# Multiply behind the reciprocal, keys' bias, a relu and a low half of the Strassen visits placed elsewhere in a fused attention and mixture-of-experts kernel

## The chip, the cores and the metric

The kernel runs on one core of a Trainium2 chip. The metric is the device time of one execution in microseconds; the median of the runs is compared. TensorE is the matmul engine, VectorE (DVE), ScalarE (ACT) and GpSimd (POOL) work on tiles, and SyncE (SP) issues most of the loads and stores.

## The reference

```python
def phi(x):                                    # x scaled by D ** -0.25
    h = einsum('bhsd,md->bhsm', x, omega) - sum(x * x, -1) / 2
    return exp(h - max(h, -1)) / sqrt(m)
q_p, k_p = phi(q), phi(k)                      # 4 batches, 8 heads, 576 tokens, 64 wide, 128 features
kv, z = einsum('bhsm,bhsd->bhmd', k_p, v), sum(k_p, 2)
x = (q_p @ kv) / (q_p @ z + 1e-6)              # 2304 tokens x 512
out = 0
for e in range(4):                             # 4 experts, 1024 hidden
    out += p[:, e] * (relu(x @ w1[e]) @ w2[e]) # p: domain_probs, normalised over the experts
```

## The kernel before

Every product of the second half is made of three matmuls in fp32r: an operand is split into a high half (rounded, by ScalarE, line 492) and a low half (the difference, by GpSimd or VectorE, line 495), and high x high, high x low and low x high are added up in a PSUM bank. `w1sh`/`w1sl`, `w1ah`/`w1al` and `w2h`/`w2l` are such pairs of weights, `xbh`/`xbl` of activations, `hh`/`hl` of the hidden layer after the relu.

The work is a list of visits (a slice of tokens, an expert and a half of its hidden units). The first slice is visited plainly (`plain`); two more slices of 896 tokens are visited eight times each by a Strassen form (`fast`): seven products `p1` to `p7` of half-blocks for each of two groups g of hidden units. Product sums live in PSUM banks (`u`, `b2`, `b5`); `keep` copies one out (line 852), and `both` adds a product to a kept sum on VectorE (line 857), applies the relu on ScalarE (`hh`, line 862) and makes the low half on VectorE (`hl`, line 863). Products 4, 6 and 7 are added onto the same bank `u`, so each waits until the reader of the one before is through. The eight visits of the last slice are deep (`DEEP`): the second layer too is done by seven products (`sevens`), with sums of w2 (`w2f`, made by `w2_sides` on GpSimd, lines 540 to 543, and split into `w2s`) and sums of hidden blocks (`t1`, `t2`, `r11`, on VectorE and GpSimd, split into `T` and, for the last, into further columns of `hs`, which the profile shows as `hl<-va,hh`).

The attention of the first batch is done ahead. That of the others, one pair of heads (`Halves`) after the other, is interleaved as steps of a generator (`later_ticks`): between parts of a visit the next step is emitted, and each engine executes what was emitted for it strictly in that order. A pair's keys are projected (`project`, `project_tails`), their maxima taken on VectorE (`maxima`, `maxima_tails`), from these and the sums of squares (`lengths`, whose squares GpSimd makes) the bias is formed (`bias`, lines 289 and 290, `nbk`), and ScalarE takes the exponentials (`exp`, `exp_tails`). These free the banks for the projection of the queries. The pair before is finished meanwhile: `numerators` (matmuls and copies to `nu` and `dn`) and `divide`, a reciprocal on VectorE (line 365) and a multiply on GpSimd into `raw_x` (line 367), the input of the expert layers.

Weights are loaded by SP into rings of few buffers (line 488); a load waits until GpSimd has made the low half of what stood in the buffer, and the loads of keys and queries (line 247) stand in the same queue behind them.

Of the kernel before, what the change touches and what calls it, by code (L numbers as in the profile page):

```python
# [14 lines left out]
def attention_moe(ctx, tc, kT, qT, kd, qd, kn, qn, vn, omT, probs, w1, w2, out):  # L15
# [10 lines left out]
    nc = tc.nc  # L26
# [42 lines left out]
    def f32(ap):  # L69
        return ap.bitcast(F32)  # L70
# [167 lines left out]
    class Halves(Pair):  # L238
# [121 lines left out]
                nc.scalar.activation(nu[own], ps[j][own], AF.Copy)  # L360
            self.num[part] = nu, dn, n

        def divide(self, part):
            nu, dn, n = self.num.pop(part)
            nc.vector.reciprocal(dn, dn)
            for o, c, m in in_ring(self.b * S + 2 * P * part, n):
                nc.gpsimd.tensor_tensor(raw_x[:, place(self.hp), c:c + m], nu[:, o:o + m], dn[:, o:o + m], ALU.mult)

# [16 lines left out]
    def later_ticks(pairs, over):  # L385

        before = None
        for p, then in zip(pairs, pairs[1:] + [None]):
            p.project("k")
            p.project_tails("k")  # L390
            p.maxima("k")
            p.maxima_tails("k")
            if before:
                before.numerators(0)
            yield
            p.bias("k")
            p.exp_tails("k")
            p.exp("k", 0)
            p.lengths("q")
            if before:  # L400
                before.divide(0)
            yield
            p.exp("k", 1)
            if before:
                before.numerators(1)
            yield
            p.project("q")
            p.project_tails("q")
            p.maxima("q")
            p.maxima_tails("q")  # L410
            p.bias("q")
            if before:
                before.divide(1)
            yield
            p.exp_tails("q")
            p.exp("q", 0)
            if then:
                then.load("k")
            yield
            p.exp("q", 1)  # L420
            if then:
                then.load("q")
            yield
            p.sum_keys()
            if then:
                then.load_v()
                if then.hp == 0:
                    then.load_tails()
                then.square("k")
            yield  # L430
            p.turn(0)
            if over and then:
                then.square("q")
            yield
            p.turn(1)
            if then:
                if over:
                    then.lengths("k")
                else:
                    then.square("q")  # L440
            yield
            if over and then:
                before = p
                continue
            before = None
            p.numerators(0)
            if then:
                then.lengths("k")
            yield
            p.divide(0)  # L450
            p.numerators(1)
            yield
            p.divide(1)
            yield

    def visit(u, n, c0, m):
# [333 lines left out]
    def start_sides2(v):  # L790
        B = {}
        g = w2_sides(v, B)
        next(g)
        sides2[v] = B, g
# [5 lines left out]
    def fast(v):  # L800
# [31 lines left out]
        def first_rows(t):  # L832
            return t[:, :WT]
# [17 lines left out]
            P_[g][name] = t = held([P, 512], "sum", F32)[:, :n]  # L851
            nc.scalar.activation(t, P_[g][where], AF.Copy)  # L852

        def both(g, f, j, where, name):
            ha, hc = (x[:, j * n:(j + 1) * n] for x in hs[2 * g + f])
            t = P_[g][name]
            nc.vector.tensor_tensor(t, P_[g][where], t, ALU.add)  # L857
            if deep and g == 0 and j == 1:
                if f == 0:
                    less(t1[:, 0], last_rows(t), r11[:, 0])  # L860
                t, ha, hc = (x[:, :n - WT] for x in (t, ha, hc))
            nc.scalar.activation(ha, t, AF.Relu)  # L862
            nc.vector.scalar_tensor_tensor(hc, t, 0.0, f32(ha), ALU.max, ALU.subtract)  # L863
            if deep and g == f == j == 0:
                nc.scalar.activation(r11[:, 0], first_rows(t), AF.Relu)

# [5 lines left out]
            product(g, 2, "b2")  # L872

        def sum2(g):
            both(g, 0, 0, "b2", "p1")

        def p5(g):
            product(g, 5, "b5")
# [10 lines left out]
        def p4(g):  # L889
            product(g, 4, "u", start=False)  # L890
            ha, hc = (x[:, :n] for x in hs[2 * g + 1])
            nc.scalar.activation(ha, P_[g]["u"], AF.Relu)  # L892
            nc.vector.scalar_tensor_tensor(hc, P_[g]["u"], 0.0, f32(ha), ALU.max, ALU.subtract)  # L893

        def p3(g):
# [16 lines left out]
        def sevens():  # L912
# [32 lines left out]
            for q in QS3:  # L945
                seventh(q, X[q][:, R], sums_of(5), mixed(1, R), start=False)
            split(r11, *T[7], nc.scalar, nc.gpsimd)
            next(ready, None)
            less(t1[:, 0], first_rows(P_[1]["p1"]), t2[:, 0])
            for q in QS3:  # L950
# [77 lines left out]
            keep_sides(v)  # L1028
        p4(0)
        if deep:  # L1030
            nc.scalar.activation(r11[:, 1], first_rows(P_[0]["u"]), AF.Relu)
            less(t1[:, 1], last_rows(P_[0]["p5"]), r11[:, 1])
            p6(1)
            split(t1, *T[5], nc.scalar, nc.gpsimd)
            if v == DEEP[0]:
                start_sides2(v + 1)
            next(ready, None)
            yield from sevens()
            return
        prepare()  # L1040
        p6(1)
        next(more, None)
        next(ready, None)
        begun(0)
        p7(1)
# [304 lines left out]
```

## Time and profile before

| | |
|---|---|
| median of the runs | 907.02 us (906.31, 907.02 and one of 1774.53) |
| profiled execution, its own time | 907.93 us |
| its span, first to last instruction | 906.2 us |
| mean granted clock of TensorE | 0.996 |
| busy: TensorE matmul, VectorE, ScalarE, GpSimd | 894.8, 581.6, 477.4, 533.4 us |

Times in the rows below are microseconds from the start of the span. A matmul's end is modelled and matmuls overlap, so the distance between two starts tells more than a row's width. In brackets stands the idle time of the engine before an instruction and what released it. L numbers are lines of the kernel before.

### The profile page before, as it was taken

How to read it: one execution, taken by the hardware profiler on the slowest of the kernel's cores; microseconds unless marked ns; L12 is line 12 of the kernel's file. 1: busy time of each engine (PE TensorE's matmuls, PEld its weight loads, DVE VectorE, ACT ScalarE, POOL GpSimd, SP SyncE). 2: the span in 40 equal slices, each digit the busy share in tenths (PEclk: the TensorE clock that was granted, in tenths of full speed). 3: DMA queues.
4: the chain of work that ended last, by engine and by line, in shares of the span. 5: the costliest groups of instructions: out<-in, count | busy, mean ns of one | idle time of the engine just before them, and what ended most of it. 6: DMA issues, size and time to landing. Idle time of an engine off the chain costs nothing.

```text
span 906.2 us, 14545 instructions
## 1 busy us (share of the span) xinstructions
PE 894.8 (99%) x5340; PEld 796.5 (88%) x5340; DVE 581.6 (64%) x985; ACT 477.4 (53%) x1077; POOL 533.4 (59%) x476
## 2 busy tenths in 40 slices
PE   9999999999999999999999999999999999999998
PEld 9888888888778888888888889888899999999998
DVE  5665567766568755474766474776756856857757
ACT  6454677776564555444455444464454544544541
POOL 4756465655534452433534333448889888898783
PEclk9999999999989999999999999999999999999999
DMA  7673444444421645234325324156333334244212
GB/s 178 162 230 118 134 157 146 152 134 155 137 70 45 214 125 180 82 117 133 117 80 194 106 92 152 59 187 209 123 110 127 113 98 152 81 130 151 82 59 82
DMA packets 57447, 117.21 MB, mean 129 GB/s; under 512 B 9824, under 2 KB 19744, under 8 KB 57376
## 3 DMA queue, kind: packets, MB, share of 16 engines
q1 hardware_dynamic: 52528, 99.21, 34.5%
q0 software_dynamic: 4608, 16.78, 5.4%
q8 instruction: 42, 0.69, 0.3%
q10 hardware_dynamic: 240, 0.30, 0.1%
q14 instruction: 29, 0.24, 0.1%
HBM read 94.77 MB, written 21.50 MB: 128 GB/s over the span
## 4 chain that ended last, share of the span: by engine, by line
PE 85%; DVE 8%; ACT 2%; issue 2%; DMA 1%; POOL 1%; SPq 0%; DVEq 0%; ACTq 0%; POOLq 0%
PE g L846 26%; PE g L910 11%; PE g L673 9%; PE g L675 9%; PE g L674 9%; PE g L658 3%; PE g L659 3%; PE g L660 3%; PE kv L314 2%; PE k_ps L266 1%; DVE hl L863 1%; DVE sum L857 1%; PE q_ps L266 1%; PE qt_ps L325 1%; PE k_ps L148 1%
## 5 line engine op out<-in xcount | busy, mean ns | idle before, releaser
L495 POOL TENSOR_TENSOR w2l<-w2r,w2h 128x512 fp32r<-128x512 f32 x93 | 120.8, 1307 | 103.7 <-ACT w2h L492 74.2
L692 DVE SCALAR_TENSOR_TENSOR acc<-g,pr,acc 128x256 f32<-128x256 f32 (+1 forms) x219 | 126.3, 603 | 45.6 <-PE g L675 31.5
L673 PE MATMUL g<-w2h,hh 128*128 128x512 f32 x344 | 138.4, 402 | 0.6 <-ACT hh L892 0.4
L675 PE MATMUL g<-w2h,hl 128*128 128x512 f32 x344 | 135.3, 393 | 0.0
L674 PE MATMUL g<-w2l,hh 128*128 128x512 f32 x344 | 135.1, 393 | 0.0
L863 DVE SCALAR_TENSOR_TENSOR hl<-sum,hh 128x448 fp32r<-128x448 f32 (+1 forms) x96 | 61.4, 639 | 105.9 <-ACT hh L862 105.9
L495 POOL TENSOR_TENSOR w1al<-w1r,w1ah 128x256 fp32r<-128x256 f32 (+1 forms) x77 | 82.6, 1089 | 48.9 <-ACT w1ah L492 45.6
L495 POOL TENSOR_TENSOR w1sl<-w1r,w1sh 128x512 fp32r<-128x512 f32 (+1 forms) x43 | 74.4, 1732 | 60.2 <-ACT w1sh L492 52.0
L862 ACT ACTIVATE hh<-sum 128x448 fp32r<-128x448 f32 (+1 forms) x96 | 50.2, 523 | 93.1 <-DVE sum L857 93.1
L846 PE MATMUL g<-xbh,w1sh 128*128 128x448 f32 x256 | 94.6, 370 | 1.5 <-ACT sum L852 1.5
L857 DVE TENSOR_TENSOR sum<-g,sum 128x448 f32<-128x448 f32 x96 | 59.5, 620 | 56.1 <-PE g L846 55.8
L846 PE MATMUL g<-xbl,w1sh 128*128 128x448 f32 x256 | 93.7, 366 | 0.0
L846 PE MATMUL g<-xbh,w1sl 128*128 128x448 f32 x256 | 93.6, 366 | 0.0
L852 ACT ACTIVATE sum<-g 128x448 f32<-128x448 f32 x96 | 51.7, 540 | 60.8 <-PE g L846 60.2
L675 PEld LDWEIGHTS g<-w2h,hl 128*128 128x128 f32 x344 | 65.0, 189 | 15.3 <-DVE hl L893 0.7
L673 PEld LDWEIGHTS g<-w2h,hh 128*128 128x128 f32 x344 | 65.2, 189 | 13.9 <-ACT hh L892 0.9
L674 PEld LDWEIGHTS g<-w2l,hh 128*128 128x128 f32 x344 | 65.2, 189 | 11.4
L846 PE MATMUL g<-xbh,w1ah 128*128 128x448 f32 x192 | 70.8, 369 | 0.7 <-DVE sum L857 0.7
L846 PE MATMUL g<-xbh,w1al 128*128 128x448 f32 x192 | 70.3, 366 | 0.0
L846 PE MATMUL g<-xbl,w1ah 128*128 128x448 f32 x192 | 70.2, 366 | 0.0
L492 ACT ACTIVATE w2h<-w2r 128x512 fp32r<-128x512 f32 x90 | 55.1, 626 | 26.8 <-DMA w2r<-in_w 14.4
L910 PE MATMUL g<-w2s,t_hl 128*128 128x256 f32 x432 | 55.2, 282 | 0.0
(198 smaller groups left out, 2222.0 us busy)
## 6 DMA issues: line engine op xcount, KB each, us to landing
w1r<-in_w SPq DMA_DIRECT2D x54, 512.0 KB, 3.6
w2r<-in_w SPq DMA_DIRECT2D x108, 256.0 KB, 2.8
kept<-w1sh SPq DMA_DIRECT2D x16, 512.0 KB, 4.8
kept<-w1sl SPq DMA_DIRECT2D x16, 512.0 KB, 5.5
w1sh<-kept POOLq DMA_DIRECT2D x16, 512.0 KB, 4.3
w1sl<-kept POOLq DMA_DIRECT2D x16, 512.0 KB, 5.0
va<-in_vn SPq DMA_DIRECT2D x14, 256.0 KB, 4.8
k<-in_kd SPq DMA_DIRECT2D x12, 288.0 KB, 3.8
```

The source lines that it names most:

```text
L492: hi.activation(a, t, AF.Copy)
L495: lo.tensor_tensor(c, t, f32(a), ALU.subtract)
L673: nc.tensor.matmul(ps, ha[:, ts_], wa, start=(c == 0), stop=False)
L674: nc.tensor.matmul(ps, ha[:, ts_], wc, start=False, stop=False)
L675: nc.tensor.matmul(ps, hc[:, ts_], wa, start=False, stop=(c == FH - 1))
L692: nc.vector.scalar_tensor_tensor(acc[i][:, cs], ps, sc, acc[i][:, cs], ALU.mult, ALU.add)
L846: nc.tensor.matmul(ps, a[:, w], x[:, k], start=(start and k + at == 0), stop=(k == 1 and at == 2), skip_group_check=not start)
L852: nc.scalar.activation(t, P_[g][where], AF.Copy)
L857: nc.vector.tensor_tensor(t, P_[g][where], t, ALU.add)
L862: nc.scalar.activation(ha, t, AF.Relu)
L863: nc.vector.scalar_tensor_tensor(hc, t, 0.0, f32(ha), ALU.max, ALU.subtract)
L910: nc.tensor.matmul(to, x, w, start=(start and f + k == 0), stop=(f + k == 3), skip_group_check=not start)
```

## The change

`divide` is taken apart: `invert` is the reciprocal, `times` the multiply, and in the steps where a next pair is under way the multiply is emitted one step later than the reciprocal. The keys' bias is emitted directly behind their maxima, before the numerators of the pair before. In `both` the low half can be held back (`hold`): outside the deep visits `sum2(1)` leaves its low half to be made by the next `both`, that of product 7 of group 0. In the deep visits the second relu for `r11` moves into `p4`, between the relu and the low half of that product; and in the first deep visit `start_sides2(v + 1)`, four sums on GpSimd, moves behind the split of `r11`. In the visits that are not deep one `next(more, None)`, a step of building the next slice's operands, goes; the step comes later.

```diff
@@ -360,9 +360,11 @@
                 nc.scalar.activation(nu[own], ps[j][own], AF.Copy)
             self.num[part] = nu, dn, n
 
-        def divide(self, part):
+        def invert(self, part):
+            nc.vector.reciprocal(self.num[part][1], self.num[part][1])
+
+        def times(self, part):
             nu, dn, n = self.num.pop(part)
-            nc.vector.reciprocal(dn, dn)
             for o, c, m in in_ring(self.b * S + 2 * P * part, n):
                 nc.gpsimd.tensor_tensor(raw_x[:, place(self.hp), c:c + m], nu[:, o:o + m], dn[:, o:o + m], ALU.mult)
 
@@ -390,18 +392,19 @@
             p.project_tails("k")
             p.maxima("k")
             p.maxima_tails("k")
+            p.bias("k")
             if before:
                 before.numerators(0)
             yield
-            p.bias("k")
             p.exp_tails("k")
             p.exp("k", 0)
             p.lengths("q")
             if before:
-                before.divide(0)
+                before.invert(0)
             yield
             p.exp("k", 1)
             if before:
+                before.times(0)
                 before.numerators(1)
             yield
             p.project("q")
@@ -410,10 +413,12 @@
             p.maxima_tails("q")
             p.bias("q")
             if before:
-                before.divide(1)
+                before.invert(1)
             yield
             p.exp_tails("q")
             p.exp("q", 0)
+            if before:
+                before.times(1)
             if then:
                 then.load("k")
             yield
@@ -447,10 +452,12 @@
             if then:
                 then.lengths("k")
             yield
-            p.divide(0)
+            p.invert(0)
+            p.times(0)
             p.numerators(1)
             yield
-            p.divide(1)
+            p.invert(1)
+            p.times(1)
             yield
 
     def visit(u, n, c0, m):
@@ -851,7 +858,9 @@
             P_[g][name] = t = held([P, 512], "sum", F32)[:, :n]
             nc.scalar.activation(t, P_[g][where], AF.Copy)
 
-        def both(g, f, j, where, name):
+        lows = []
+
+        def both(g, f, j, where, name, hold=False):
             ha, hc = (x[:, j * n:(j + 1) * n] for x in hs[2 * g + f])
             t = P_[g][name]
             nc.vector.tensor_tensor(t, P_[g][where], t, ALU.add)
@@ -860,7 +869,11 @@
                     less(t1[:, 0], last_rows(t), r11[:, 0])
                 t, ha, hc = (x[:, :n - WT] for x in (t, ha, hc))
             nc.scalar.activation(ha, t, AF.Relu)
-            nc.vector.scalar_tensor_tensor(hc, t, 0.0, f32(ha), ALU.max, ALU.subtract)
+            lows.append((hc, t, ha))
+            if not (hold and not deep):
+                for x, y, z in lows:
+                    nc.vector.scalar_tensor_tensor(x, y, 0.0, f32(z), ALU.max, ALU.subtract)
+                lows.clear()
             if deep and g == f == j == 0:
                 nc.scalar.activation(r11[:, 0], first_rows(t), AF.Relu)
 
@@ -872,7 +885,7 @@
             product(g, 2, "b2")
 
         def sum2(g):
-            both(g, 0, 0, "b2", "p1")
+            both(g, 0, 0, "b2", "p1", hold=g == 1)
 
         def p5(g):
             product(g, 5, "b5")
@@ -890,6 +903,8 @@
             product(g, 4, "u", start=False)
             ha, hc = (x[:, :n] for x in hs[2 * g + 1])
             nc.scalar.activation(ha, P_[g]["u"], AF.Relu)
+            if deep and g == 0:
+                nc.scalar.activation(r11[:, 1], first_rows(P_[0]["u"]), AF.Relu)
             nc.vector.scalar_tensor_tensor(hc, P_[g]["u"], 0.0, f32(ha), ALU.max, ALU.subtract)
 
         def p3(g):
@@ -945,6 +960,8 @@
             for q in QS3:
                 seventh(q, X[q][:, R], sums_of(5), mixed(1, R), start=False)
             split(r11, *T[7], nc.scalar, nc.gpsimd)
+            if v == DEEP[0]:
+                start_sides2(v + 1)
             next(ready, None)
             less(t1[:, 0], first_rows(P_[1]["p1"]), t2[:, 0])
             for q in QS3:
@@ -1028,18 +1045,14 @@
             keep_sides(v)
         p4(0)
         if deep:
-            nc.scalar.activation(r11[:, 1], first_rows(P_[0]["u"]), AF.Relu)
             less(t1[:, 1], last_rows(P_[0]["p5"]), r11[:, 1])
             p6(1)
             split(t1, *T[5], nc.scalar, nc.gpsimd)
-            if v == DEEP[0]:
-                start_sides2(v + 1)
             next(ready, None)
             yield from sevens()
             return
         prepare()
         p6(1)
-        next(more, None)
         next(ready, None)
         begun(0)
         p7(1)
```

GpSimd's list at the place in the last plain visits where a pair's keys are loaded late, before. `raw_x` is the multiply, `w2l`, `w1al`, `w1sl` and `sum` are low halves of weights, `k` and `q` squares:

```order
L495 TENSOR_TENSOR w1sl<-w1r,w1sh 128x512 x2
L367 TENSOR_TENSOR raw_x<-nu,dn 128x256
L495 TENSOR_TENSOR w1al<-w1r,w1ah 128x512
L495 TENSOR_TENSOR w1sl<-w1r,w1sh 128x512
L367 TENSOR_TENSOR raw_x<-nu,dn 128x320
L495 TENSOR_TENSOR w2l<-w2r,w2h 128x512 x4
L251 TENSOR_TENSOR k<-k 128x576
L251 TENSOR_TENSOR q<-q 128x576
```

and after the change:

```order
L502 TENSOR_TENSOR w1sl<-w1r,w1sh 128x512 x2
L502 TENSOR_TENSOR w1al<-w1r,w1ah 128x512
L369 TENSOR_TENSOR raw_x<-nu,dn 128x256
L502 TENSOR_TENSOR w1sl<-w1r,w1sh 128x512
L502 TENSOR_TENSOR w2l<-w2r,w2h 128x512 x2
L369 TENSOR_TENSOR raw_x<-nu,dn 128x320
L502 TENSOR_TENSOR w2l<-w2r,w2h 128x512 x2
L251 TENSOR_TENSOR k<-k 128x576
L251 TENSOR_TENSOR q<-q 128x576
```

The first multiply has gone behind one low half, the second behind two, in front of which it stood.

VectorE's list in the first half of a Strassen visit that is not deep, before. `sum<-g` are the additions of `both`, in the order of products 2 (both groups), 7 and 3, `hl` the low halves:

```order
L857 TENSOR_TENSOR sum<-g_3644,sum 128x448
L863 SCALAR_TENSOR_TENSOR hl<-sum,hh 128x448
L857 TENSOR_TENSOR sum<-g_3686,sum 128x448
L863 SCALAR_TENSOR_TENSOR hl<-sum,hh 128x448
L857 TENSOR_TENSOR sum<-g_3629,sum 128x448
L863 SCALAR_TENSOR_TENSOR hl<-sum,hh 128x448
L857 TENSOR_TENSOR sum<-g_3651,sum 128x448
```

and after:

```order
L866 TENSOR_TENSOR sum<-g_3644,sum 128x448
L875 SCALAR_TENSOR_TENSOR hl<-sum,hh 128x448
L866 TENSOR_TENSOR sum<-g_3686,sum 128x448
L866 TENSOR_TENSOR sum<-g_3629,sum 128x448
L875 SCALAR_TENSOR_TENSOR hl<-sum,hh 128x448 x2
L866 TENSOR_TENSOR sum<-g_3651,sum 128x448
```

The addition of product 7 (`g_3629`) stands directly behind that of product 2 of the second group, and their two low halves follow.

GpSimd's list in the second half of the first deep visit, before. `w2f` are the sums of w2, `r` is `r11`, the two DMAs fetch kept weights:

```order
L495 TENSOR_TENSOR t_hl<-va,t_hl 128x768
L540 TENSOR_TENSOR w2f<-w2r 128x256
L541 TENSOR_TENSOR w2f<-w2f,w2r 128x256
L542 TENSOR_TENSOR w2f<-w2r,w2f 128x256
L543 TENSOR_TENSOR w2f<-w2r 128x256
L625 DMA w1sh<-kept 128x1024
L625 DMA w1sl<-kept 128x1024
L941 TENSOR_TENSOR r_6651<-vb,r_6651 128x768
L495 TENSOR_TENSOR t_hl<-r_6651,t_hl 128x768
L495 TENSOR_TENSOR w1al<-w1r,w1ah 128x512
```

and after:

```order
L502 TENSOR_TENSOR t_hl<-va,t_hl 128x768
L632 DMA w1sh<-kept 128x1024
L632 DMA w1sl<-kept 128x1024
L956 TENSOR_TENSOR r_6651<-vb,r_6651 128x768
L502 TENSOR_TENSOR t_hl<-r_6651,t_hl 128x768
L547 TENSOR_TENSOR w2f<-w2r 128x256
L548 TENSOR_TENSOR w2f<-w2f,w2r 128x256
L549 TENSOR_TENSOR w2f<-w2r,w2f 128x256
L550 TENSOR_TENSOR w2f<-w2r 128x256
L502 TENSOR_TENSOR w1al<-w1r,w1ah 128x512
```

The four sums have gone behind `r11` and its low half. Behind this piece both lists go on with the rest of w1al, two more fetches and `hl<-va,hh`.

## Rows read from the trace of the kernel before

**Rows 1.** The page's busy table, TensorE: busy us, share, instructions

```profile
PE 894.8 (99%) x5340; PEld 796.5 (88%) x5340; DVE 581.6 (64%) x985; ACT 477.4 (53%) x1077; POOL 533.4 (59%) x476
```

**Rows 2.** Waits of TensorE: total us, times, longest

```profile
PE g L846 <- ACT sum L852: 1.5, 7, 0.2
...
PE g L846 <- DVE sum L857: 0.7, 2, 0.4
...
PE g L910 <- DVE hl L893: 0.6, 1, 0.6
PE g L673 <- ACT hh L892: 0.4, 1, 0.4
```

**Rows 3.** Windows, 240 to 260 us: busy by engine, granted clock, DMA

```profile
240.00:260.00 20.00, 18.37 (x94) 14.40 (x93) 15.68 (x25) 13.59 (x37) 9.02 (x9) 0.83 0.35 110
```

**Rows 4.** Timeline of TensorE near 250 us: start, us, tile [idle before, releaser]

```profile
249.35 1.54 PE L266 MATMUL q_ps<-om_r,q 64*128 64x128 f32 x16 [0.63 <-ACT kp L303]
...
252.84 0.79 PE L658 MATMUL g<-xh,w1sh 128*128 128x512 f32 x1
```

**Rows 5.** Chain of waits from 236 to 262 us: start, us, what

```profile
238.81 5.87 DMA q<-in_qn
...
248.73 0.18 DVE nbk L290
...
253.63 0.43 PE g L659
...
259.25 0.23 PE g L673
```

**Rows 6.** Timeline of SP's DMA issues near 237 us

```profile
237.50 0.33 SPq L247 DMA_DIRECT2D k<-in_kd  x1
```

**Rows 7.** Timeline of GpSimd near 233 us

```profile
233.35 0.87 POOL L367 TENSOR_TENSOR raw_x<-nu,dn 128x320 f32<-128x320 f32 x1 [2.77 <-DVE dn L365]
```

**Rows 8.** Timeline of TensorE, one pair of heads earlier

```profile
201.50 0.39 PE L675 MATMUL g<-w2h,hl 128*128 128x512 f32 x1
...
203.24 1.16 PE L266 MATMUL q_ps<-om_r,q 64*128 64x128 f32 x16
...
204.56 0.50 PE L673 MATMUL g<-sum,hh 128*128 128x512 f32 x1
```

**Rows 9.** Timeline of VectorE and TensorE near 404 us

```profile
401.09 0.60 DVE L284 TENSOR_REDUCE mxk<-t_ps 64x1 f32<-64x128 f32 x2
...
404.29 0.17 DVE L290 SCALAR_TENSOR_TENSOR nbk<-sqk,mxk 128x9 f32<-128x9 f32 x1
...
404.97 0.49 PE L274 MATMUL t_ps<-om_r,q 64*128 64x128 f32 x2 [0.64 <-ACT kp L303]
```

**Rows 10.** Timeline of ScalarE, VectorE and TensorE, second deep visit

```profile
668.91 0.55 ACT L892 ACTIVATE hh<-g 128x448 fp32r<-128x448 f32 x1 [0.30 <-PE g L846]
670.75 0.49 ACT L1031 ACTIVATE r<-g 128x384 f32<-128x384 f32 x1 [1.30 <-DVE hl L893]
...
670.11 0.61 DVE L893 SCALAR_TENSOR_TENSOR hl<-g,hh 128x448 fp32r<-128x448 f32 x1
...
671.24 0.28 PE L910 MATMUL g<-w2h,hl 128*128 128x256 f32 x1
671.73 0.47 PE L846 MATMUL g<-xbh,w1sh 128*128 128x448 f32 x1 [0.22 <-ACT sum L852]
```

**Rows 11.** Timeline of GpSimd and TensorE, first deep visit; r of the second

```profile
643.15 1.87 POOL L941 TENSOR_TENSOR r<-vb,r 128x768 f32<-128x768 f32 x1
...
651.04 2.00 POOL L495 TENSOR_TENSOR hl<-va,hh 128x384 fp32r<-128x384 f32 x2
...
654.99 0.28 PE L910 MATMUL g<-w2h,hl 128*128 128x256 f32 x1
...
678.27 1.86 POOL L941 TENSOR_TENSOR r<-vb,r 128x768 f32<-128x768 f32 x1 [2.27 <-DVE vb L830]
```

**Rows 12.** Windows of w2f's instructions alone: ACT, POOL busy (x), clock, DMA

```profile
638.00:643.00 5.00, 0.00 (x0) 3.89 (x4) 1.00 0.00 0
```

## The prediction

> **What bounds the kernel now.** The page's busy table comes first: TensorE's matmuls fill 99% of the span [rows 1]. The other engines can therefore matter only where they make TensorE wait, so the next view is the waits, for TensorE alone [rows 2]: single microseconds, in few places. But a wait there counts only the idle time, not the slower start behind it or a lowered clock. So I next read the windows with the granted clock. One stretch stands out: from 240 to 260 us the mean clock is 0.83 [rows 3], whereas over the whole run it is 0.996. There the time goes to something other than matmuls at full rate.
>
> **The large stall, followed backwards.** TensorE's query projection waits 0.63 us at 249.35 for a bank that ScalarE's key exponentials release, and ordinary matmuls resume only at 252.84 [rows 4]. From there the chain of waits shows steps of 0.43 us for a 128x512 matmul that takes 0.23 us in the same chain further on, which is the 1.2 GHz level in place of 2.4. The same chain says why the exponentials were late: they need the keys' bias (nbk, 248.73), which follows the sum of squares, which follows a load that landed 5.87 us after its issue at 238.81 [rows 5]. The loads of the keys ahead of it on SP's queue were issued from 237.50 on [rows 6]. SP had weight loads ahead of them that wait for GpSimd's w2l subtractions to free their buffers, and GpSimd stood still for 2.77 us with its multiply at the head of its queue, waiting for VectorE's reciprocal [rows 7]. So a wait on GpSimd, 15 us earlier, becomes a wait of TensorE. This is the place to cost first.
>
> **The change part by part.** Nothing is removed: all matmuls, their order and SP's order stay. Only waits can go. The sum is made against the profiled execution's own 907.93 us; the median of the runs is 907.02.
>
> *GpSimd's multiply one step later.* At this place two w2l now stand ahead of the multiply. I take them as ready, since ScalarE's queue has their w2h ahead of the queries' exponentials, so they use the idle 2.77 us, and with the multiply's own 0.87 the first w2l moves up by up to 3.6 us. SP's weight loads and the keys' loads follow by as much, and the bias with them, to about 245.5 us; TensorE wants the bank at 248.7. What the stall costs: 0.63 wait; the block from the query projection to the next matmul takes 252.84 − 249.35 = 3.49 us, while the same block elsewhere takes 204.56 − 203.24 = 1.32 [rows 4, 8], so 2.17 more; twelve steps of 0.43 in place of 0.23 (253.63 to 258.75 in the chain, [rows 5]), so 2.4; some 0.4 in the first slow step. Together 5.6 us. VectorE's reciprocal stays ahead of the hl that frees the second bank, so I keep 0.4 as a residue: **−5.2**. The same order stands one pair earlier (185 to 203 us), where four matmul steps take 203.24 − 201.50 = 1.74 us in place of 4 x 0.23 [rows 8]: 0.8 at most, **−0.6**. The price of the later multiply: raw_x is written some 2 us later, and its readers come only with the sums of the second stage; nothing on TensorE waits for it now, and the buffers of nu and dn are wanted again only four steps later. I cost it at nothing.
>
> *Keys' bias directly behind their maxima.* At 401.69 the maxima are done, but the bias is written only at 404.46, behind an accumulate and four additions; TensorE meanwhile waits 0.64 us for the tail's bank [rows 9]. With the bias 2.4 us earlier that wait goes with its slow restart: **−0.8** (between 0.64 and 1.1). The accumulate slips by two instructions of 0.17 us; nobody waits for it here.
>
> *The low half held back (hold).* In the eight Strassen visits of the first slice VectorE now does the addition for product 7 directly behind that of product 2, and two hl afterwards. Where VectorE is late, TensorE waits for that addition: 0.7 us in two places, and once 0.4 us for hh of product 4 behind the same queue [rows 2]. With three slower starts 1.5 us; moving one building step out of the visit helps the last. **−1.4**. In the visits where VectorE is not late it gains nothing. What it delays, hl of product 2, is read only after the visit's first half.
>
> *The relu of r in the deep visits.* ScalarE's r relu waits 1.30 us for VectorE's hl of the same bank. The next activation, which frees the bank for product 7, follows behind it, and TensorE's product 7 starts at 671.73 where the step before it, at 671.24, takes 0.12: about 0.37 us lost [rows 10], in each of the seven visits where [rows 2] counts that wait. Placed directly behind hh (ends 669.46) the relu ends near 669.9. Now hl must wait for it instead; but VectorE starts hl at 670.11 anyway [rows 10]. So nothing is added on the critical side: six later visits x 0.37 = **−2.2**.
> The Trainium skill (PSUM — Partial Sum Buffer, "PSUM bank collisions raise a hardware error") says two engines may not touch one bank and quadrant at once, reads included, and that nothing in the chip arbitrates. So the order of these two readers is a real dependency, which the move turns round and does not remove. The trace agrees: r starts 0.03 us after hl ends. If all of r's 0.49 us fell on hl, and from there on TensorE, it would be more than the 0.37 won, and this term would be nothing.
>
> *The four w2f sums of the first deep visit moved behind r and its halves.* Before, they run between t_hl and r and take 3.89 us [rows 12]. In that visit they slow VectorE, and TensorE waits for its hl (0.6 us, [rows 2]). Without them there, up to 1.4 us comes back, with the relu's 0.3. But now they stand ahead of w1al and of hl<-va, which the visit's last matmuls need. That hl ends at 653.04 and the first matmul that needs the second of them starts at 654.99: 1.95 us of slack [rows 11]. 3.9 us are put ahead of it, less what r gains: r starts at 643.15 and was not waiting for its input, so it moves up by perhaps 1 to 1.5 us, until it waits for vb, as the later visits' r does for 2.27 us [rows 11]. So hl comes 2.4 to 2.9 us later, 0.5 to 1 us too late, and what the visit gains at its middle it gives back at its end: **+0.3** (from −1.4, if GpSimd keeps up, to +2.9, if the sums are slowed to 5.5 us).
> The Trainium skill (SBUF — State Buffer, "Who interferes with whom") says that GpSimd is blocked only by VectorE instructions with two SBUF inputs or in a two-port mode. Beside the moved sums VectorE reads PSUM, so by that page they would take some 3 us, and the term would be −0.5. No row here shows w2f beside only such work.
>
> Sum: −5.2 − 0.6 − 0.8 − 1.4 − 2.2 + 0.3 = −9.9 us. From 907.93 that is 898.0, and from the median 907.02 it is **897.1 us**; I say 897.0.
>
> **Rivals.**
> *The keys' loads come no earlier.* If SP's weight loads wait for something else than w2l (a landed load, or w2h), the two terms of the multiply are lost. For it: the 5.87 us of landing are the memory's and stay. Against: SP's first weight load there follows the first w2l directly. 907.0 − 4.1 = 902.9 us.
> *A lowered clock in the first deep visit.* If the new wait of about 1 us at its end is followed by a fall of the clock like the one at 252 us, 2.8 us are added: about 900 us. Against: the wait of 0.64 us at 404.97 brought no fall [rows 9].
> *GpSimd never catches up (slower).* The deep visits are GpSimd's fullest. If the 3.9 us put behind r are not regained in the second visit, every visit's hl<-va comes late, by about 3.9 − 1.95 = 2 us, eight times: 16 us, of which the other parts' gains (8.0) pay half: 915 us. It decides from the point where GpSimd's idle time per visit is below the lateness; the 2.27 us in front of r alone take up most of it [rows 11], so I give it little.
> *The waits go but others end as late.* VectorE's and ScalarE's chains behind the banks stay; if each gap shrinks only by half, 902 us.
>
> **How the numbers follow.** The forecast: 0.65; the loads no earlier or half gains: 0.20; the clock: 0.08; GpSimd late throughout: 0.05; other: 0.02. The forecast's best bounds are 0.8 + 6.0 + 1.1 + 1.6 + 2.2 + 1.4 = 13.1, so 893.9; the first rival ends at 902.9. The range is 893.8 to 903.2. Two per cent are 18 us, about what a measurement of this kernel can tell from no change. TensorE's idle time is 906.2 − 894.8 = 11.4 us, and the slow stretch and slower starts add some microseconds; not all of it can go, so faster by over 2% has 0.01, slower by over 2% (GpSimd late in every visit with falls of the clock) 0.02, within 2% 0.97.
>
> **What would show it.** Right: the window that holds the slow stretch has the clock at 1.00; the keys' loads are issued some 3.5 us earlier after the weight loads; no wait of product 7 on the activation in the deep visits; no tail wait near 404. Right on the loss: a wait of TensorE for GpSimd's hl<-va at the end of the first deep visit. Wrong: the clock still falls near 250 us, or waits for hl<-va in the later visits.

## The result

| | before | after |
|---|---|---|
| median of the runs, timed together | 906.43 us | 897.32 us |
| their range | 906.1 to 907.02 us, and one of 1774.53 | 896.42 to 897.92 us |
| profiled execution, its own time | 907.93 us | 896.99 us |
| its span | 906.2 us | 895.2 us |

The ratio is 0.9898, with a 95% interval of 0.9882 to 0.9914: 9.1 us less, between 7.8 and 10.7. It is within two per cent and clearly not nothing. The forecast was 897.0, or 9.9 us less. The total is close; three of its terms are not.

The busy table of the changed kernel, the row that answers to [rows 1]:

```profile
PE 886.4 (99%) x5340; PEld 792.5 (89%) x5340; DVE 577.5 (65%) x985; ACT 478.2 (53%) x1077; POOL 532.1 (59%) x476
```

The instructions are as many as before. TensorE's busy time is 8.4 us less with the same matmuls, so most of what went was not idle time in this table: a matmul that starts slowly or runs at the lower clock counts as busy. TensorE's waits after, as in [rows 2] (total us, times, longest):

```profile
PE k_ps L148 <- DVE k L141: 1.1, 1, 1.1
...
PE g L925 <- DVE hl L908: 1.0, 1, 1.0
PE g L682 <- DVE hl L672: 0.8, 1, 0.8
...
PE g L925 <- POOL hl L502: 0.3, 1, 0.3
```

The seven waits for ScalarE's `sum` and the two for VectorE's `sum` are gone. The first row is at the start of the program, in the first batch's attention, and changes from execution to execution (0.4 in the second profile of before, 0.2 in a kernel with all edits and the sums early). The other three are new, and each has a place below. The windows of the changed kernel, the first of them the stretch of [rows 3] (busy by engine, granted clock, DMA share, GB/s):

```profile
240.00:260.00 20.00, 19.22 (x126) 15.83 (x126) 14.59 (x25) 14.45 (x39) 9.83 (x9) 1.00 0.31 94
...
640.00:650.00 10.00, 9.65 (x69) 9.12 (x69) 5.38 (x12) 2.33 (x4) 9.99 (x12) 1.00 0.63 202
```

In 240 to 260 us TensorE now does 126 matmuls where it did 94, at a clock of 1.00 in place of 0.83. Next is the timeline of the changed kernel at that place, in order SP, GpSimd, TensorE and VectorE (start, us, engine and tile, in brackets the idle time before and its releaser):

```profile
233.30 0.33 SPq L247 DMA_DIRECT2D k<-in_kd  x1
...
229.98 2.52 POOL L502 TENSOR_TENSOR w2l<-w2r,w2h 128x512 fp32r<-128x512 f32 x2
234.67 0.88 POOL L369 TENSOR_TENSOR raw_x<-nu,dn 128x320 f32<-128x320 f32 x1 [2.17 <-DVE dn L364]
...
247.81 1.16 PE L266 MATMUL q_ps<-om_r,q 64*128 64x128 f32 x16
...
249.13 0.50 PE L665 MATMUL g<-xh,w1sh 128*128 128x512 f32 x1
...
252.88 0.39 PE L681 MATMUL g<-w2l,hh 128*128 128x512 f32 x1
254.06 0.50 PE L682 MATMUL g<-w2h,hl 128*128 128x512 f32 x1 [0.78 <-DVE hl L672]
...
251.13 2.15 DVE L364 RECIPROCAL dn<-dn 128x320 f32<-128x320 f32 x1
253.31 0.69 DVE L672 SCALAR_TENSOR_TENSOR hl<-g,hh 128x512 fp32r<-128x512 f32 x1
```

The two w2l stand ahead of the multiply, the keys' load goes out at 233.30 in place of 237.50 [rows 6], and the block from the query projection to the next ordinary matmul takes 1.32 us in place of 3.49 [rows 4]. GpSimd still stands still in front of the multiply (2.17 us), but the keys' loads wait for nothing behind it; two further `w2l`, and the weight loads that wait for them, still stand there. What is late next shows in the last four rows: the reciprocal takes 2.15 us on VectorE, an `hl` stands behind it, and TensorE waits for that `hl`. Two steps that are 0.23 us apart elsewhere are 1.18 apart there, so 0.95 us are lost again.

### The profile page after: what moved, and what is told of

The parts are those of the page before. It is cut to its first block, busy times and chain, and to the rows that moved or that the text cites. A ratio compares the mean times of both kernels' runs of the same rounds, so it can differ in the third digit from the quotient of the medians.

```text
span 895.2 us, 14533 instructions
## 1 busy us (share of the span) xinstructions
PE 886.4 (99%) x5340; PEld 792.5 (89%) x5340; DVE 577.5 (65%) x985; ACT 478.2 (53%) x1077; POOL 532.1 (59%) x476
## 4 chain that ended last, share of the span: by engine, by line
PE 94%; DVE 3%; POOL 1%; issue 1%; DMA 1%; ACT 1%; SPq 0%; DVEq 0%; ACTq 0%
PE g L853 28%; PE g L925 13%; PE g L680 10%; PE g L682 10%; PE g L681 10%; PE g L665 3%; PE g L667 3%; PE g L666 3%; PE kv L314 2%; PE q_ps L266 1%; PE k_ps L266 1%; PE qt_ps L325 1%; PE nd L353 1%; PE k_ps L148 1%; PE kv L178 1%; PE nd L355 1%
```

## The experiments

TensorE's order is the same in all these kernels, so the starts of one and the same matmul can be compared between two traces. "Lead" below is how much earlier it starts than in the profiled execution of before; the change of the lead over a stretch is what that stretch gained, and the times of a stretch are those of before's profile. Medians are over the runs of a kernel, each beside runs of before on the same chip.

| kernel | median us | before us | ratio, 95% interval |
|---|---|---|---|
| multiply alone | 902.31 | 905.45 | 0.9960 (0.9948 to 0.9972) |
| bias alone | 903.50 | 905.45 | 0.9980 (0.9967 to 0.9992) |
| hold alone | 904.15 | 905.45 | 0.9982 (0.9969 to 0.9996) |
| relu alone | 902.75 | 905.45 | 0.9969 (0.9956 to 0.9983) |
| sums alone | 906.64 | 906.47 | 1.0008 (0.9993 to 1.0024) |
| keys' loads early, nothing else | 902.51 | 906.47 | 0.9954 (0.9939 to 0.9969) |
| all but the sums' move | 895.55 | 906.47 | 0.9872 (0.9850 to 0.9895) |
| all, the sums early | 895.26 | 906.47 | 0.9874 (0.9854 to 0.9894) |
| all but the multiply's split | 900.53 | 906.16 | 0.9939 (0.9921 to 0.9958) |
| all, sums early, reciprocal late | 894.01 | 906.16 | 0.9865 (0.9850 to 0.9880) |

**The multiply alone.** The kernel before, with `divide` split and the multiply one step later (an excerpt; the multiply of a pair's first part, `times(0)`, moves one step in the same way):

```diff
-                before.divide(1)
+                before.invert(1)
             yield
             p.exp_tails("q")
             p.exp("q", 0)
+            if before:
+                before.times(1)
```

> The kernel before with the multiply one step behind the reciprocal, and nothing else of the change. Theory: the weight loads and with them the keys' loads come earlier, so the gain of the stretch from 190 to 260 us stands here alone: TensorE ahead by about 5.9 us at 262 us (0.7 at 203, the rest at 248 to 259, clock 1.00 there) and no further on; 906.5 - 5.9 = 900.6 us. Rival (the bias placed earlier is what lets the exponentials come in time): the slow stretch stays, at most 0.7 us gained, 905.8 us.

Measured 902.31, 3.1 us less. The keys' load goes out at 232.72 and the stop is gone. The lead grows by 4.5 us from 247.5 to 263 us (from 1.52 to 6.03), as in the changed kernel (0.84 to 5.35). But the medians give 3.1, and my terms said 5.8. The next experiments show most of the reason.

**The bias alone.**

```diff
             p.maxima_tails("k")
+            p.bias("k")
             if before:
                 before.numerators(0)
             yield
-            p.bias("k")
```

> The kernel before with the keys' bias directly behind the maxima, alone. Theory: only the stop near 404 us goes, 1.1 to 1.4 us with its slow restart; the slow stretch at 252 us stays with its clock of one half, since there the bias already stands directly behind the maxima; about 905.2 us. Rival (the bias is what ended the slow stretch): about 900 us and a clock of 1.00 between 240 and 260 us.

Measured 903.50, 2.0 us less (0.7 to 3.0 by the interval). At its own place the lead grows by 1.1 us (3.65 at 400 us, 4.76 at 410): the tail's wait and the slow start behind it. What I had not foreseen is that the lead also grows by 2.5 us between 247.5 and 263 us (1.26 to 3.74), where this kernel has no edit that helps. Its window and its timeline of TensorE there:

```profile
250.00:260.00 10.00, 8.89 (x46) 7.33 (x47) 7.29 (x11) 8.52 (x24) 5.99 (x5) 1.00 0.12 29
```

```profile
247.82 1.54 PE L266 MATMUL q_ps<-om_r,q 64*128 64x128 f32 x16 [0.36 <-ACT kp L303]
...
250.59 0.48 PE L274 MATMUL t_ps<-om_r,q 64*128 64x128 f32 x2 [0.73 <-DVE hl L665]
251.00 0.50 PE L658 MATMUL g<-xh,w1sh 128*128 128x512 f32 x1
251.34 0.39 PE L659 MATMUL g<-xl,w1sh 128*128 128x512 f32 x1
251.57 0.40 PE L660 MATMUL g<-xh,w1sl 128*128 128x512 f32 x1
...
255.69 0.50 PE L675 MATMUL g<-w2h,hl 128*128 128x512 f32 x1 [0.52 <-DVE hl L665]
```

The stop is there, with two waits and a block of 251.00 − 247.82 = 3.18 us. But the steps behind it are 0.23 us, and the clock is 1.00. In the profile of before the same steps took 0.43, twelve times over. So the stop comes without the lowered clock too. The wait for `hl` at 255.69, too, is hidden in the profile of before, where everything behind the stop is late.

**The hold alone** (an excerpt; `sum2` passes `hold=g == 1`, and the building step stays in the visit).

```diff
-            nc.vector.scalar_tensor_tensor(hc, t, 0.0, f32(ha), ALU.max, ALU.subtract)
+            lows.append((hc, t, ha))
+            if not (hold and not deep):
+                for x, y, z in lows:
+                    nc.vector.scalar_tensor_tensor(x, y, 0.0, f32(z), ALU.max, ALU.subtract)
+                lows.clear()
```

> The kernel before with the low half held back until product 7 is added, alone, without the building step taken out. Theory: 0.5 to 0.9 us at the first Strassen visit (305 us) and 0.5 to 1.2 us at the eighth (593 to 598 us), nothing in the six between; 905 us. Rival (the building step is what makes VectorE late in the eighth): no gain at 593 to 598 us, 905.8 us.

Measured 904.15, 1.3 us less. At the two places of the `sum` waits the lead grows by 0.7 us (302 to 310 us) and 1.3 us (590 to 602 us). The changed kernel gains 0.8 and 1.3 there, so the hold makes these gains by itself; at these places the building step adds nothing that shows.

**The relu alone** (an excerpt; the same call is taken from behind `p4(0)`).

```diff
             nc.scalar.activation(ha, P_[g]["u"], AF.Relu)
+            if deep and g == 0:
+                nc.scalar.activation(r11[:, 1], first_rows(P_[0]["u"]), AF.Relu)
             nc.vector.scalar_tensor_tensor(hc, P_[g]["u"], 0.0, f32(ha), ALU.max, ALU.subtract)
```

> The kernel before with the relu of r moved ahead of the low half in the deep visits, alone. Theory: TensorE gains 0.48 us in each of the visits from the second to the seventh and 0.3 to 0.5 in the first, no loss in the second: about 3.0 us, 903.4 us. Rival (the bank's second reader only moves the wait to the low half): TensorE waits for that low half instead and less than 1 us is gained, 905.5 us.

Measured 902.75, 2.7 us less (1.5 to 4.0 by the interval). The lead grows by 0.47 us in each of the six later deep visits that had the wait and by 1.0 us in the first (0.43 of it at product 7), and no visit loses.

**The four sums alone.**

```diff
             split(r11, *T[7], nc.scalar, nc.gpsimd)
+            if v == DEEP[0]:
+                start_sides2(v + 1)
```

(and the same call taken from behind the split of `t1`).

> The kernel before with the four sums of the first deep visit moved behind r and its halves, alone. Theory: a loss in all: 0.6 to 0.9 us come back in the middle of the first deep visit, 0.3 to 1 us go at its end, where the last matmuls wait for GpSimd, and 1 to 1.5 us in the second, where GpSimd is late, its next sums run beside VectorE's instructions on two operands in SBUF and TensorE waits for a low half: 907 to 907.5 us. Rival (the move only frees VectorE): 905.6 us and no wait in the second deep visit.

Measured 906.64, no gain: the ratio leaves room from 0.6 us faster to 2.2 slower. The trace tells more than the medians. The lead grows by 1.3 us in the middle of the first deep visit (3.58 at 602 us, 4.89 at 652), falls by 0.8 at its end (to 4.10), and by another 1.5 in the second deep visit (to 2.61 at 674), where TensorE waits 1.0 us for VectorE's `hl`. Together 1.0 us is lost.

**All but the sums' move**, that is the changed kernel with `start_sides2(v + 1)` back behind the split of `t1`.

> The changed kernel with these four sums back at their old place. Theory: the waits of 0.34 and 1.04 us in the first two deep visits go, the one of 0.6 us for the low half in the first comes back; 0.8 to 1.3 us faster than the changed kernel, 896.2 us. Rival (the wait in the second visit comes from the relu's new place): it stays, and the kernel is as slow as the changed one or slower by 0.6, 897.3 to 898 us.

Measured 895.55, about 1.8 us below the changed kernel's 897.32 (which ran on another occasion; the ratios to before, 0.9872 and 0.9898, differ by 2.4 us). The waits for `hl<-va` and for 1.0 us of `hl` in the second visit are not there.

**All, with the sums early**: they stand directly behind `p4(0)`, ahead of `less` and of the split of `t1` (an excerpt; the call behind the split of `r11` is taken out).

```diff
         p4(0)
         if deep:
+            if v == DEEP[0]:
+                start_sides2(v + 1)
             less(t1[:, 1], last_rows(P_[0]["p5"]), r11[:, 1])
             p6(1)
             split(t1, *T[5], nc.scalar, nc.gpsimd)
```

> The changed kernel with these four sums emitted earlier, ahead of the split that GpSimd waits 3 us for in the first deep visit. Theory: they run in that idle time, so neither the middle nor the end of this visit nor the second visit waits; 1.3 to 1.8 us faster than the changed kernel, 895.7 us. Rival (they come before their weights have landed, or before VectorE's own low halves are through, and make the split late): a new wait of TensorE for the split's products, 0.5 to 2 us, 897 us.

Measured 895.26. It can't be told from the one before by its time. So the old place was as good as this one, and the new place is the bad one.

**The keys' loads early, and nothing else.** A rival to the multiply: the kernel before, where only `load("k")` of the next pair is emitted one step earlier, so that SP has it ahead of the weight loads. GpSimd's order stays.

```diff
                 before.divide(1)
+            if then:
+                then.load("k")
             yield
             p.exp_tails("q")
             p.exp("q", 0)
-            if then:
-                then.load("k")
```

> The kernel before, the multiply where it was, with only the keys' load of the next pair emitted one step earlier, so that on SP's queue it stands ahead of the weight loads that wait for GpSimd. Theory (the keys' load was late because of what stood before it on its queue): the slow stretch goes without any change on GpSimd, TensorE ahead by 4 to 5.5 us at 262 us, 901.5 us. Rival (the gain came from GpSimd's or VectorE's own earlier work): the stretch stays, 906.4 us.

The timeline of SP in this kernel:

```profile
230.34 0.79 SPq L247 DMA_DIRECT2D k<-in_kd  x1
...
234.77 1.57 SPq L488 DMA_DIRECT2D w2r<-in_w  x2
```

The weight loads go out only at 234.77, where the multiply alone has them at 230.72; the keys' loads go out 7 us earlier than in [rows 6], and the lead at 247.5 to 263 us grows by 4.5 us, as with the multiply. Measured 902.51, 4.0 us less, where the multiply alone gave 3.1 with an interval of 2.5 to 4.7. So at this place the multiply works through the keys' loads, and nothing shows that the weights' earlier arrival adds to it.

**All but the multiply's split**: the changed kernel with the reciprocal and multiply together again.

> The changed kernel with the multiply back directly behind the reciprocal, the other three edits kept. If the multiply is worth here what it is worth alone (3.1 us between the medians): 900.4. If its share grows because nothing else covers the stop at 250 us (my prediction's 5.2 and 0.6): 903. If the other edits make its place unimportant: 898 or less. The profile should show the keys' loads issued at about 237 us again, the stop near 249 us, and its granted clock tells once more whether the stop brings a lower clock (1.00 by theory 1 of the kernel before).

Measured 900.53, 3.2 us above the changed kernel (by the ratios to before, 3.7). So the multiply is worth as much beside the other parts as alone, within the intervals. The stop is back, with the clock at 1.00.

**The kernel before once more.** It is the same code.

> The kernel before itself, profiled once more. Theory 1 (the lowered clock at 250 to 259 us belonged to that one execution; the stop of TensorE belongs to the kernel): the wait of about 0.6 us for the query projection's bank and the long step behind it are there again, the granted clock of the window from 240 to 260 us is 1.00, and the span is some 2.4 us below 906.2. Theory 2 (the stop brings the lower clock with it): the window shows 0.83 again and the span is within 1 us of 906.2.

The window of this execution, and its timeline of TensorE one pair earlier and at the stop:

```profile
250.00:260.00 10.00, 9.27 (x40) 7.55 (x39) 8.40 (x12) 8.68 (x24) 5.36 (x5) 0.83 0.27 91
```

```profile
201.98 0.39 PE L675 MATMUL g<-w2h,hl 128*128 128x512 f32 x1
...
202.99 0.38 PE L266 MATMUL q_ps<-om_r,q 64*128 64x128 f32 x2
...
250.91 0.49 PE L274 MATMUL t_ps<-om_r,q 64*128 64x128 f32 x2 [0.73 <-DVE hl L665]
251.32 0.79 PE L658 MATMUL g<-xh,w1sh 128*128 128x512 f32 x1
251.92 0.63 PE L659 MATMUL g<-xl,w1sh 128*128 128x512 f32 x1
...
254.05 0.63 PE L673 MATMUL g<-w2h,hh 128*128 128x512 f32 x1
```

Neither theory is right as it stood. The clock did fall again, but later and for a shorter time: six steps of 0.43, until 254.5 us, at a stop that lacks the first wait (the query projection starts at 248.14 without one). The span is 903.6, 2.6 us less. So behind the same code the clock stays low for twelve steps (mean granted clock 0.996) or for six (0.998). A mean does not tell where the clock fell, but it gives an idea of how often. These are all 56 timed executions of before that ran beside these kernels:

| mean granted clock | executions | median us |
|---|---|---|
| 1.00 | 33 | 905.32 |
| 0.999 | 6 | 905.50 |
| 0.998 | 10 | 906.49 |
| 0.996 | 7 | 908.25 |

The profiled execution that I predicted from has 0.996 and 907.93 us: it belongs with the seven of the lowest clock, and is 2.6 us above the median of the 33 at 1.00. In the 36 executions of the kernels whose keys' loads come early (the multiply alone, the keys early, the three combinations without the stop, and the changed kernel) the mean clock was never below 0.999. But it was not below 0.999 either in the ten executions of the bias alone and the four of all but the multiply's split, whose keys' loads come late and whose profiles have the stop; in the hold, the relu and the sums alone, which have neither the split nor the early bias, it was below in 12 of 30. So the early loads are not the only edit that goes with a full clock, and what the early bias does there was not tried. The rows one pair earlier put my second term in doubt as well: the stretch of [rows 8] takes 202.99 − 201.98 = 1.01 us here, where it took 1.74, without any edit.

**All, the sums early, and the reciprocal late.** The changed kernel's new wait for `hl` behind the reciprocal suggested one more step: the reciprocal of a pair's second part (`invert(1)`) one step later, and its multiply one step later again (an excerpt; the sums' move is shown further up).

```diff
-                before.invert(1)
             yield
             p.exp_tails("q")
             p.exp("q", 0)
             if before:
-                before.times(1)
+                before.invert(1)
             if then:
                 then.load("k")
             yield
             p.exp("q", 1)
+            if before:
+                before.times(1)
```

> The changed kernel with the four w2f sums early (directly behind p4(0)), and with the second pair's reciprocal one step later on VectorE, its multiply one step later again. Theory (the new 0.95 us gap near 253 us comes from the reciprocal of 2.15 us that stands on VectorE ahead of the hl that frees a bank): the wait for hl (L672) near 253 us goes, 894.4 us, 0.9 below the kernel with the sums early alone. Rival A (another instruction of VectorE's queue is late next, or the reciprocal only blocks an hl further on): as with the sums early alone, 895.3. Rival B (the later multiply holds up GpSimd's subtractions and the loads of the queries or the keys behind them): 896 or more.

Measured 894.01, the best of all: 1.2 us below the kernel with the sums early, and 3.3 us below the changed kernel (3.0 by the ratios to before, 0.9865 and 0.9898). Its window and its timeline of VectorE:

```profile
240.00:260.00 20.00, 20.00 (x133) 16.92 (x132) 15.42 (x26) 15.88 (x40) 9.82 (x9) 1.00 0.29 90
```

```profile
251.04 0.69 DVE L672 SCALAR_TENSOR_TENSOR hl<-g,hh 128x512 fp32r<-128x512 f32 x1 [0.23 <-ACT hh L671]
...
253.78 2.14 DVE L364 RECIPROCAL dn<-dn 128x320 f32<-128x320 f32 x1
```

The `hl` comes ahead of the reciprocal, and TensorE is busy for all 20 us of the window. Neither rival came: nothing else is late there, and the later multiply holds up nothing that TensorE waits for.

## Why the prediction was right, and where it was not

*The multiply (−5.2): mechanism right, size wrong.* Each link held: two w2l ahead of the multiply, SP's weight and keys' loads 4.2 us earlier, the bias with them, no wait for the projection. The last link, through the keys' loads, is confirmed by the kernel that moves nothing else. The size was wrong because the sum took the twelve steps at the lowered clock (2.4 us) as the kernel's. Without them the trace gives 4.5 us less the 2.1 to 2.5 that five kernels with the stop still in them gain there as well (bias, hold, relu and sums alone, all but the multiply): 2.0 to 2.4. The clock falls in a part of the executions, which adds about 0.6 us in the mean. It does not explain why the medians say 3.1 and 3.2: beside the multiply alone the 25 executions of before with a mean clock of 0.999 or more have a median of 905.27, still 3.0 us above it, and the four of the kernel with all but the split are all at 1.00. So 0.6 to 1.2 us between the trace and the medians have no place. The residue for `hl` behind the reciprocal was foreseen as 0.4 and is 0.95, but in the bias alone, which has the stop, the same step (to 255.69) is 0.7 us late as well.

*One pair earlier (−0.6): not shown.* The changed kernel gains 0.74 there, but so do before's second profile and the bias alone, without the edit. Of the seven profiles whose keys' loads come late, four have 1.01 to 1.05 us for the stretch of [rows 8], the hold alone has 1.31, the relu alone 1.73 and the first profile of before 1.74; all six with the early loads have 1.01. So the lateness comes and goes without the edit, and whether the edit keeps it away stays open. The sum took what one execution showed.

*The bias (−0.8): right, somewhat more.* 1.1 us (1.0 in the changed kernel), the upper end of its bounds. The keys' tails of the changed kernel at the place of [rows 9], VectorE's bias and then TensorE:

```profile
396.02 0.17 DVE L290 SCALAR_TENSOR_TENSOR nbk<-sqk,mxk 128x9 f32<-128x9 f32 x1
...
397.74 0.39 PE L274 MATMUL t_ps<-om_r,q 64*128 64x128 f32 x4
398.06 0.50 PE L680 MATMUL g<-w2h,hh 128*128 128x512 f32 x1
```

*The hold and the building step (−1.4): right, too small.* 2.1 us in the changed kernel. TensorE's three waits there are 1.1 us together, as I had them, but the hold alone gains 0.6, 0.6 and 0.7 us at them (306.24, 593.73 and 597.57 us in the profile of before). So the slower starts cost some 0.8 us and not the 0.4 that I took. The building step I credited with a part of this shows no part.

*The relu (−2.2 in six visits): right, too small.* The second deep visit of the changed kernel, ScalarE and TensorE, the rows that answer to [rows 10]:

```profile
661.01 0.48 ACT L907 ACTIVATE r<-g 128x384 f32<-128x384 f32 x1
...
663.17 0.28 PE L925 MATMUL g<-w2h,hl 128*128 128x256 f32 x1
663.30 0.36 PE L853 MATMUL g<-xbh,w1sh 128*128 128x448 f32 x1
```

Product 7 follows after 0.13 us in place of 0.49, and its first matmul takes 0.36 in place of 0.47: 0.47 us per visit, not 0.37. I had left out that first slow matmul, a thing I had counted at the other places. Six visits make 2.8. That VectorE's `hl` must now wait for the relu cost nothing, as argued.

*The four sums (+0.3): wrong in one step.* The first visit went as worked out: 1.4 us come back by the end of its middle (0.8 of them at the old wait; a part is the relu's), and with a wait for `hl<-va` 0.8 go at its end. GpSimd and TensorE of the changed kernel there:

```profile
632.42 1.86 POOL L956 TENSOR_TENSOR r<-vb,r 128x768 f32<-128x768 f32 x1 [2.45 <-DVE vb L837]
...
637.24 0.73 POOL L547 TENSOR_TENSOR w2f<-w2r 128x256 f32<-128x256 f32 x1
638.06 0.74 POOL L548 TENSOR_TENSOR w2f<-w2f,w2r 128x256 f32<-128x256 f32 x1
638.88 0.73 POOL L549 TENSOR_TENSOR w2f<-w2r,w2f 128x256 f32<-128x256 f32 x1
639.57 0.74 POOL L550 TENSOR_TENSOR w2f<-w2r 128x256 f32<-128x256 f32 x1
...
643.31 1.99 POOL L502 TENSOR_TENSOR hl<-va,hh 128x384 fp32r<-128x384 f32 x2
...
645.36 0.39 PE L925 MATMUL g<-w2h,hl 128*128 128x256 f32 x1 [0.34 <-POOL hl L502]
```

The sums take 2.9 us of GpSimd's time here, where they took 3.89 [rows 12]. The Trainium skill (SBUF — State Buffer, "Who interferes with whom") says that a VectorE instruction with at most one input in SBUF, outside the two-port modes, does not contend with GpSimd. The trace agrees: beside the sums here VectorE reads PSUM and not two tiles from SBUF. But the −0.5 that I drew from the rule for the term did not come, because the loss lies elsewhere: in "what the visit gains at its middle it gives back at its end" I stopped at the end of that visit. GpSimd enters the second one late. ScalarE, GpSimd, VectorE and TensorE of the changed kernel there:

```profile
657.76 0.63 ACT L499 ACTIVATE w2s<-w2f 128x512 fp32r<-128x512 f32 x1 [1.36 <-POOL w2f L549]
658.30 0.24 ACT L871 ACTIVATE hh<-sum 128x64 fp32r<-128x64 f32 x1
...
658.47 2.57 POOL L502 TENSOR_TENSOR w2s<-w2f,w2s 128x512 fp32r<-128x512 f32 x2
...
658.64 1.22 DVE L875 SCALAR_TENSOR_TENSOR hl<-sum,hh 128x64 fp32r<-128x64 f32 x1 [0.97 <-ACT hh L871]
...
662.05 0.61 DVE L908 SCALAR_TENSOR_TENSOR hl<-g,hh 128x448 fp32r<-128x448 f32 x1
...
661.39 0.28 PE L925 MATMUL g<-w2l,hh 128*128 128x256 f32 x1
662.72 0.38 PE L925 MATMUL g<-w2h,hl 128*128 128x256 f32 x1 [1.04 <-DVE hl L908]
```

The same instructions in the kernel with all but the sums' move, ScalarE, GpSimd and VectorE:

```profile
657.15 0.61 ACT L499 ACTIVATE w2s<-w2f 128x512 fp32r<-128x512 f32 x1
...
657.84 1.32 POOL L502 TENSOR_TENSOR w2s<-w2f,w2s 128x512 fp32r<-128x512 f32 x1 [0.46 <-ACT w2s L499]
...
658.89 0.35 DVE L875 SCALAR_TENSOR_TENSOR hl<-sum,hh 128x64 fp32r<-128x64 f32 x1 [0.45 <-ACT hh L871]
...
661.71 0.61 DVE L908 SCALAR_TENSOR_TENSOR hl<-g,hh 128x448 fp32r<-128x448 f32 x1
```

GpSimd's late `w2f` holds ScalarE's split of it for 1.36 us; the next `hh` stands behind that split; VectorE's `hl` of it is late, and beside GpSimd's `w2s` it takes 1.22 us in place of 0.35, where it meets only the end of one. The `hl` (L908) that TensorE needs is behind all of this. The cost is 1.5 us. So the term is about +0.9 in place of +0.3, as in the kernel with the sums alone (+1.0). Against the kernel with all but the sums' move, in which the first visit gains 0.7 us as well, the move costs 1.5 us by the trace.

*The rivals.* The keys' loads did come earlier, so the first fell. No fall of the clock came behind the wait at 645.36 (the window of 640 to 650 us has 1.00). GpSimd did fall late for a second visit, as the third rival had it, but caught up there: in that visit's second half it waits 2.26 us for `vb` again, as before [rows 11]. The fourth fell for the bias, the hold and the relu, whose gains came whole; behind the multiply something else did end late, the `hl`.

*The sum.* Measured by places: multiply 2.2 and, as a mean over executions, about 0.6 for the clock (seven of 56 by 2.9 us and ten by 1.2, against 905.32); bias 1.1; hold 2.1; relu 2.8; sums −0.9 (with the relu's share in the first visit). That is 7.9, against 9.1 between the medians; the 1.2 us that are left have no place, and the interval of the result is ±1.4. The medians of the five kernels with one part each add up to 8.9 (3.1 + 2.0 + 1.3 + 2.7 − 0.2), so the parts neither help nor hinder one another by much. By places, two terms were too large by 3.0 us, three too small by 1.6, and the sums' loss too small by 0.6. So the right total (9.9 forecast, 9.1 measured) is partly luck: errors of both signs, and a remainder on the forecast's side.

## What to carry to other kernels

A profile is one execution. Before a stall's whole cost is put into a sum, look at how that execution's clock stands to the other runs' (0.996 against 1.00 here): what a stop costs and what the clock adds behind it are two terms, and the second has to be weighed with how often it comes. When work is put later on a filled engine, follow its lateness into the next round of the loop, through each queue that takes its results, and not only to the end of the round where it was moved.

## What was not expected of the hardware

The clock of TensorE behind one and the same stop: with waits of 0.63 and 0.73 us it fell for twelve steps of 0.43, with 0.73 alone in another execution for six, and with 0.7 and 0.7 in the profile of the hold alone not at all (1.00 in its window from 250 to 260 us). The length of the stop does not sort these three. What does was not tried.

A VectorE instruction of 128x64 with two operands from SBUF (`hl<-sum,hh`) takes 0.21 us with GpSimd idle beside it (at 633.42 in the profile of before). In the changed kernel it starts 0.17 us behind the start of GpSimd's subtraction of 128x512 (1.3 us) and takes 1.22 us; in the kernel with all but the sums' move it starts 0.27 us ahead of the end of one and takes 0.35. In both it ends 0.08 us behind GpSimd's instruction. So here it stood until that was through, and what it lost depended on when it began. The section of the Trainium skill named above says that a VectorE instruction with two inputs in SBUF contends with a GpSimd instruction that reads SBUF. The traces agree; I had weighed it for the sums alone and not for so short a neighbour.
